# Spectral mixing and a max-of-two MLP: z read back by thirds, exchange reads spread, one batch's stores on SyncE

## The chip, the cores and the metric

The kernel runs on one core of a Trainium2 chip. The metric is the device time of one execution in microseconds. Before the change three runs took 501.76, 507.77 and 511.94 us; their median is 507.77.

The core's engines are TensorE (PE; its weight loads are shown as PEld), VectorE (DVE), ScalarE (ACT), GpSimd (POOL) and SyncE (SP). SyncE computes nothing here: it issues transfers, one after another, in the order in which the program names them, and a transfer that must wait holds up those behind it on that queue.

## The reference

Each of 8 batches of `x` (3072 positions x 256 channels) is transformed along the positions, multiplied by a complex filter and transformed back; every position then passes through an MLP whose hidden value is the larger of two products.

```python
def _attn_ref(x, filt_r, filt_i):
    X = np.fft.rfft(x, axis=1)
    F = (filt_r + 1j * filt_i)[None, :, :]
    Y = X * F
    y = np.fft.irfft(Y, n=x.shape[1], axis=1)
    return y.astype(np.float32)

def _moe_ref(x, w1, w2, w_out):
    h1 = x @ w1
    h2 = x @ w2
    g = np.maximum(h1, h2)
    return (g @ w_out).astype(np.float32)
```

There are 24576 tokens, 256 channels and 1024 hidden units.

## The kernel before, in words

**The transform.** 3072 is 96 x 32, and each batch goes through four small matrix stages with an exchange through DRAM between them. S1 (`s1`, L350) multiplies along 96; its result goes to a DRAM tile `ad` (L372) and comes back in another order as `bt` (`s1_read`, L374: the exchange reads, six per batch, two transfers each). S2 (`s2_pairs`, L445) multiplies along 32; its result times the filter (L464, DVE) is added up to real and imaginary parts on GpSimd (`add_pairs`, L482: L485, L486). S3 (`s3_pairs`, L489) transforms back along 32, in three thirds k = 0, 1, 2 of 8 blocks u each; ACT and DVE copy its result to `zt`, and SyncE writes it to the DRAM tile `zd` with two transfers (L507). The `zd` rows come back in yet another order as `zr`, the z of the change's name (`z_read3`, L381 to L386). S4 (`s4g`, L542, matmuls L549) transforms back along 96. Three tiles of S4 are formed at once: at step 61 of a batch those of the next batch's columns m = 0 to 11, at the next batch's step 4 those of m = 12 to 23, at its step 25 the rest. Each needs all 24 blocks u.

**The MLP.** max(a, b) = b + max(a - b, 0), so one product with w1 - w2 (`Wd`) and a relu do (`moe_h`, L585 to L592), and the w2 branch is folded into a 256 x 256 matrix `M`. `moe_o` (L625) sums ten matmuls per 128 tokens (L640 with `M`, L642 with `Wo`), DVE copies the sum to `ot` (L653), and `out_block` (L597, L601) stores it. `VS` (L580) lists the steps whose relu is on DVE and not on ACT.

**The order.** Everything runs in one schedule written by hand (L912 to L936). A batch is 8 tiles of 384 tokens, a tile has 8 steps, so a batch has 64 steps. At each step TensorE does one of 8 hidden chunks of tile tt (`moe_h`) and about 3 to 7 of the 30 output matmuls of tile tt - 1 (`share`, L896); at some steps a group of transform work for the next batches stands between them (`groups`, L861 to L872: S3 of a third, S2 of a sixth, S1 of some of 8 chunks of x). At a step with a group three of the output matmuls are done ahead of it and the others behind it. `plan(b, step, fn, ...)` hangs a function on the end of a step (`todo`); a step of 64 or more lies in the next batch, a negative one in the batch before. What the functions issue goes to the queues in that order. Batches 1 to 6 (L862) prepare batches 2 to 7 this way; batch 0 prepares batch 1 by other functions.

SyncE's queue in such a batch holds 16 x loads (`load_xf`, L97), 8 S1 writes, 12 exchange reads, 6 z writes, 8 z reads and the stores that GpSimd doesn't issue. x comes into three buffers `XF` in turn; GpSimd adds and subtracts its halves (`fold`, L107, L108), and `load_xf` waits until its buffer has been folded.

**z now.** S3 of the last third is in the group of step 44. `z_read3(b, u0, u1, m)` reads blocks u0 to u1 and 16 of the 32 columns m, in two transfers, one for each s. At step 46 it reads u 0 to 16, at step 47 u 16 to 24, both for m under 16; at steps 54 and 56 the same for m from 16. For u 0 to 16 a transfer has 32 rows of 8 KB (256 KB), for u 16 to 24 it has 16 rows of 8 KB (128 KB).

**Stores now.** Tiles 0 to 7 are stored by GpSimd; of the others up to the last two, the blocks of even number 3 tt + c by GpSimd and those of odd number by SyncE.

Of the kernel before, what the change touches and what calls it, by code (L numbers as in the profile page):

```python
# [13 lines left out]
B = 8  # L14
# [13 lines left out]
def kernel(  # L28
# [14 lines left out]
    nc = tc.nc  # L43
    V, S, G, TE = nc.vector, nc.scalar, nc.gpsimd, nc.tensor
# [276 lines left out]
    zr = {}  # L321
    ad = {}
    zd = {}
# [54 lines left out]
            src = ad[b][48 * r:48 * r + 48].rearrange("(u r) m d -> (r m) u d", r=2)  # L378
            nc.sync.dma_start(out=bt[b][64 * r:64 * r + 64, 4 * v:4 * v + 4], in_=src[:, 4 * v:4 * v + 4])  # L379

    def z_read3(b, u0, u1, m):  # L381
        if b not in zr:
            zr[b] = zrpool.tile([128, NM, D], BF16, tag="zr", name="zr")
        src = zd[b][u0:u1].rearrange("u (s r m) d -> s u r m d", s=2, r=2)
        for s in range(2):
            nc.sync.dma_start(out=zr[b][64 * s + 2 * u0:64 * s + 2 * u1, m:m + 16], in_=src[s][:, :, m:m + 16])  # L386

    def z_read(b, h, ms=(0, 16)):
        if b not in zr:
# [15 lines left out]

    def product(E, v, s, px, pool=None):
        pq = (pool or pqpool).tile([128, 2, 2, D], BF16, tag="pq", name="pq")
        E.tensor_tensor(pq, px.rearrange("p (o i) d -> p o i d", o=1).to_broadcast([128, 2, 2, D]),  # L408
                        F[:, :, 2 * v:2 * v + 2, s], OP.mult)
        return pq  # L410
# [166 lines left out]
            if (j in (1, 4, 6) if 2 < 8 * i + j < 11 else j in (1, 2, 4, 6, 7) if 8 * i + j < 22  # L577
                else (j in (1, 5) and (i, j) != (3, 1)) or (i, j) == (3, 0) if 8 * i + j < 48 else j in (1, 3, 6) and (i, j) != (7, 6))}

    VS = (1, 3, 8, 13, 18, 24, 28, 30, 34, 38, 44, 46, 48, 50, 52, 54, 56, 58, 60)  # L580

    def moe_h(tt, j):
        if j == 0:
# [3 lines left out]
        for dc in range(2):  # L587
            TE.matmul(ph, Wd[:, dc, 128 * j:128 * j + 128], y_[:, dc], start=(dc == 0), stop=(dc == 1))  # L588
        if (tt, j) in on_v if tt < 8 else 8 * (tt % 8) + j in VS if tt < 8 * B - 8 else j in (1, 3, 6):
            V.tensor_scalar(gt[tt][:, j], ph, 0.0, None, OP.max)  # L590
# [6 lines left out]
    def out_block(tt, c):  # L597
        b, i = divmod(tt, 8)
        dst = out[b * N:(b + 1) * N].rearrange("(c p i m) d -> c i p (m d)", c=3, p=32, i=8)[c, i]
        E = G if tt < 8 or (tt < 8 * B - 2 and (3 * tt + c) % 2 == 0) else nc.sync  # L600
        E.dma_start(out=dst, in_=ot[tt // 2][:, 3 * (tt % 2) + c])  # L601


    def last_block(tt):
        y_, g_ = yt[tt], gt[tt]
        dst = out[tt // 8 * N:(tt // 8 + 1) * N].rearrange("(c p i m) d -> c i p m d", c=3, p=32, i=8)[2, tt % 8]
        for cols, E in ((slice(0, 176), S), (slice(176, D), V)):
            pl = ps.tile([128, cols.stop - cols.start], FP32, tag="ps", name="pl")
# [5 lines left out]
            o_ = ot[tt // 2][:, 5, cols]  # L614
            if E is S:
                S.activation(o_, pl, AF.Copy, scale=SCALE)
# [8 lines left out]
    def moe_o(tt, k0, k1):  # L625
        y_, g_ = yt[tt], gt[tt]
        for k in range(k0, k1):
            c, e = divmod(k, 10) if tt else FIRST[k]
            n = e if tt else (e + 2) % 10
            q = 3 * tt + c  # L630
            blk = slice(128 * c, 128 * c + 128)
            if q == 24 * B - 1:
                if e == 0:
                    last_block(tt)
                continue
            if e == 0 and q % 2 == 0:
                po[q // 2 % 2] = pso.tile([128, 2, D], FP32, tag="po", name="po")
            p_ = po[q // 2 % 2][:, q % 2]
            if n < 2:
                TE.matmul(p_, y_[:, n, blk], M[:, n], start=(e == 0), stop=(e == 9))  # L640
            else:
                TE.matmul(p_, g_[:, n - 2, blk], Wo[:, n - 2], start=(e == 0), stop=(e == 9))  # L642
            if e == 9 and q == 24 * B - 2:
                S.activation(ot[tt // 2][:, q % 6], p_, AF.Copy, scale=SCALE)
                out_block(tt, c)
            elif e == 9 and q % 2 == 1:
                if q % 6 == 1:
                    ot[tt // 2] = opool.tile([128, 6, D], FP32, tag="ot", name="ot")
                e = q % 6
                if tt < 8:  # L650
                    V.tensor_copy(ot[tt // 2][:, e - 1:e + 1], po[q // 2 % 2])
                else:
                    V.tensor_scalar(ot[tt // 2][:, e - 1:e + 1], po[q // 2 % 2], SCALE, None, OP.mult)  # L653
                for qq in (q - 1, q):
                    out_block(qq // 3, qq % 3)
# [173 lines left out]
    def plan(b, step, fn, *a):  # L829
        todo.setdefault((b + step // 64, step % 64), []).append((fn, a))  # L830
# [31 lines left out]
    for b in range(1, B - 1):  # L862
        first = b == 1
        plans = [(9, 0, None, (0, 1)), (14, 1, None, (2, 3)), (20, 2, None, (4,)), (30, 3, 0, ()),
                 (34, 4, None, (5, 6)), (38, 5, 1, ()), (44, None, 2, (7,))]
        if first:
            plans = [(10, 0, None, (0, 1)), (15, 1, None, (2,)), (20, 2, None, (3,)), (30, 3, 0, ()),
                     (34, 4, None, (4, 5)), (38, 5, 1, ()), (44, None, 2, (6,)), (50, None, None, (7,))]
        for st, n, k, quads in plans:
            groups[b, st] = (b + 1, n, k, quads)  # L870
            if n is not None and n < 5:
                plan(b, st + 3, add_pairs, b + 1, n)  # L872
        for n, u0, u1, m in ((46, 0, 16, 0), (47, 16, 24, 0), (54, 0, 16, 16), (56, 16, 24, 16)):
            plan(b, n, z_read3, b + 1, u0, u1, m)
        if b + 2 < B:
            xs, folds = (((-30, -23, -9, -3, 4, 11, 18, 25), (-24, -17, -2, 4, 11, 18, 25, 32)) if first
                         else ((-34, -28, -22, -14, -6, 2, 9, 16), range(-22, 34, 7)))
            for c in range(8):
                plan(b, xs[c], load_xf, b + 2, c)
                plan(b, folds[c], fold, b + 2, c)  # L880
            for v, n in enumerate((57, 61, 65, 69, 73, 78) if first else (53, 58, 63, 68, 73, 78)):
                plan(b, n, s1_read, b + 2, v)
    for k, n in enumerate((47, 50, 53, 56, 59)):
        plan(0, n, to_pairs, k)
# [12 lines left out]
    for b in range(B + 1):  # L897
        for i in range(8):
            at = [j for j in range(8) if (b, 8 * i + j) in group or (b, 8 * i + j) in groups]
            if at:  # L900
                n = [6 if j in at else 3 for j in range(8)]
# [3 lines left out]
            else:  # L905
                n = [4, 4, 4, 3, 4, 4, 4, 3]
# [5 lines left out]
    for tt in range(8 * B + 1):  # L912
        b, i = divmod(tt, 8)
        k = 0
        for j in range(8):
# [5 lines left out]
            n = share[b, i][j]  # L921
            if (b, step) in group or (b, step) in groups:
# [5 lines left out]
                k, n = k + 3, n - 3  # L928
# [38 lines left out]
```

## Time and profile before

| | |
|---|---|
| runs | 501.76, 507.77, 511.94 us |
| profiled execution | 509.6 us |
| its span, first to last instruction | 507.8 us |
| mean granted TensorE clock | 0.990 |
| DVE, ACT, POOL busy | 72%, 61%, 59% |
| HBM read, written | 53.87 MB, 47.19 MB |

In the timelines a row gives start and duration in us, engine, line, operation, out<-in and the count of instructions put together in it; what stands in brackets is the engine's idle time ahead of it and what ended that. SPq is SyncE's queue; there the duration includes waiting among the instructions of the row. In the view of waits the three numbers are us in total, times, and the longest in us. In the windows view the columns are the stretch, its length, busy time (and count) of PE, PEld, DVE, ACT and POOL, the granted clock, the mean busy share of the 16 DMA engines, and GB/s.

Batch b begins its step 61, where the first z of the next batch is wanted, at about 158.9 (b = 1), 215.6, 273.0, 336.7 and 395.7 us.

### The profile page before, as it was taken

What the parts mean: (1) busy time and instruction counts of PE and PEld (TensorE: products, weight loads), DVE (VectorE), ACT (ScalarE), POOL (GpSimd) and SP (SyncE); (2) the same over time, 40 slices, a digit from 0 to 9 for tenths busy, and PEclk for the clock granted to TensorE, in tenths of its full rate; (3) what the DMA queues carried; (4) which work ended last, traced back from release to release, by engine and by line L of the source; (5) the groups of instructions that cost most, each with busy time, mean ns of one, the idle gap of its engine ahead of it and who ended that gap; (6) DMA issues with size and microseconds to landing.
All of it is one profiled execution on the core that took longest, in us unless ns stands there. A gap on an engine that the chain in (4) does not pass through costs nothing.

```text
span 507.8 us, 15399 instructions
## 1 busy us (share of the span) xinstructions
PE 484.1 (95%) x6204; PEld 344.2 (68%) x6207; DVE 364.0 (72%) x601; ACT 310.1 (61%) x651; POOL 299.3 (59%) x381
## 2 busy tenths in 40 slices
PE   8689999999899999999998699999999999999997
PEld 3457777776567676767676476766767766777775
DVE  7876787877676878578775487757786788766543
ACT  5777478766564767467764377646774555554432
POOL 8794868558975695749774287755961055311110
PEclk9889999999999999999999899999999999999999
DMA  8999999996688957998589775898657732651212
GB/s 129 155 238 222 252 258 266 274 246 203 168 236 247 243 161 208 273 244 237 153 228 230 170 216 146 236 241 209 201 150 204 209 105 86 187 160 61 72 65 83
DMA packets 85368, 97.37 MB, mean 192 GB/s; under 512 B 8945, under 2 KB 65682, under 8 KB 83922
## 3 DMA queue, kind: packets, MB, share of 16 engines
q1 hardware_dynamic: 75842, 77.34, 56.0%
q0 software_dynamic: 9312, 18.98, 14.9%
q8 instruction: 48, 0.79, 0.7%
q14 instruction: 22, 0.18, 0.1%
q10 hardware_dynamic: 144, 0.09, 0.1%
HBM read 53.87 MB, written 47.19 MB: 199 GB/s over the span
## 4 chain that ended last, share of the span: by engine, by line
PE 61%; DMA 8%; SPq 2%; issue 1%; DVE 0%; ACT 0%; DVEq 0%
PE po L642 24%; PE ph L588 23%; DMA zr<-zd 8%; PE po L640 6%; PE pa L365 2%; PE pz L498 2%; PE px L454 2%; PE pc L549 1%; SPq L386 1%; SPq L601 0%; DVE gt L590 0%; ACT ce L554 0%; PE pl L613 0%; SPq L379 0%; DVE y__9395 L556 0%
## 5 line engine op out<-in xcount | busy, mean ns | idle before, releaser
L642 PE MATMUL po<-Wo,gt 128*128 128x256 bf16 x1528 | 264.1, 274 | 0.0
L592 ACT ACTIVATE gt<-ph 128x384 bf16<-128x384 f32 x352 | 167.9, 502 | 134.3 <-PE ph L588 132.9
L642 PEld LDWEIGHTS <-gt 128*128 128x128 bf16 x1528 | 144.8, 98 | 67.5 <-issue 12.2
L601 POOL DMA_DIRECT2D out_dram<-ot x105 | 59.6, 568 | 137.6 <-DVE ot L653 128.2
L590 DVE TENSOR_SCALAR gt<-ph 128x384 bf16<-128x384 f32 x160 | 88.4, 553 | 48.5 <-PE ph L588 47.3
L588 PEld LDWEIGHTS <-Wd 128*128 128x128 bf16 x1024 | 99.3, 98 | 16.2 <-POOL Wd L301 0.8
L464 DVE TENSOR_TENSOR pf<-px,F 128x1024 f32<-128x1024 f32 x60 | 71.4, 1219 | 24.3 <-PE px L454 9.5
L107 POOL TENSOR_TENSOR xb<-XF 128x512 bf16<-128x512 f32 x48 | 61.1, 1272 | 43.7 <-DMA XF<-in_x_dram 18.9
L653 DVE TENSOR_SCALAR ot<-po 128x512 f32<-128x512 f32 x83 | 56.9, 686 | 20.2 <-PE po L642 19.8
L108 POOL TENSOR_TENSOR xb<-XF 128x512 bf16<-128x512 f32 x48 | 61.7, 1285 | 0.0
L369 ACT ACTIVATE at<-pa 128x512 bf16<-128x512 f32 x96 | 50.7, 606 | 6.7 <-PE pa L365 6.1
L485 POOL TENSOR_TENSOR ri<-pf 128x256 bf16<-128x256 f32 x60 | 43.6, 727 | 9.5 <-DVE pf L464 9.2
L506 ACT ACTIVATE zt<-pz 128x512 bf16<-128x512 f32 x60 | 31.3, 601 | 20.4 <-PE pz L498 20.4
L486 POOL TENSOR_TENSOR ri<-pf 128x256 bf16<-128x256 f32 x60 | 43.4, 723 | 0.0
L554 ACT ACTIVATE ce<-pc 128x384 f32<-128x384 f32 x56 | 24.1, 490 | 13.2 <-PE pc L549 12.0
L408 DVE TENSOR_TENSOR pq<-px,F 128x1024 bf16<-128x1024 f32 x19 | 22.2, 1219 | 4.5 <-PE px L402 2.2
L549 PE MATMUL pc<-G,zr 48*128 48x48 bf16 x896 | 16.5, 181 | 9.3 <-DMA zr<-zd 9.2
L549 PEld LDWEIGHTS <-zr 48*128 48x128 bf16 x896 | 13.5, 93 | 14.6 <-issue 10.1
L365 PE MATMUL pa<-xb,CT 64*32 64x512 bf16 x320 | 17.6, 383 | 0.0
L454 PE MATMUL px<-bt,U 64*32 64x256 bf16 x432 | 14.8, 273 | 0.4 <-DVE gt L590 0.4
L724 PE MATMUL pd<-W 128*128 128x512 bf16 x28 | 9.9, 468 | 1.5 <-DVE zero L153 1.5
L476 DVE TENSOR_TENSOR pf<-px,F 128x512 f32<-128x512 f32 x12 | 8.2, 686 | 4.2 <-issue 4.2
(408 smaller groups left out, 733.7 us busy)
## 6 DMA issues: line engine op xcount, KB each, us to landing
XF<-in_x_dram SPq DMA_DIRECT2D x96, 192.0 KB
out_dram<-ot POOLq DMA_DIRECT2D x105, 128.0 KB, 3.7
out_dram<-ot SPq DMA_DIRECT2D x86, 128.0 KB
ad<-at SPq DMA_DIRECT2D x56, 192.0 KB
zd<-zt SPq DMA_DIRECT2D x42, 256.0 KB
bt<-ad SPq DMA_DIRECT2D x72, 128.0 KB
zr<-zd SPq DMA_DIRECT2D x24, 256.0 KB
zr<-zd SPq DMA_DIRECT2D x24, 128.0 KB
```

What stands on the lines that cost most here:

```text
L107: G.tensor_tensor(t_[:, 0], f[:, 0], f[:, 1], OP.add)
L108: G.tensor_tensor(t_[:, 1], f[:, 0], f[:, 1], OP.subtract)
L369: S.activation(at[:, m0:m0 + 2], pa[g], AF.Copy)
L464: V.tensor_tensor(t_, px[s].rearrange("p (o k) d -> p o k d", o=1).to_broadcast([128, 2, 2, D]), F[:, :, 2 * n, s].rearrange("p c (o d) -> ...
L485: G.tensor_tensor(ri[:, s, 0], t_[:, 0, 0], t_[:, 1, 1], OP.subtract)
L486: G.tensor_tensor(ri[:, s, 1], t_[:, 0, 1], t_[:, 1, 0], OP.add)
L588: TE.matmul(ph, Wd[:, dc, 128 * j:128 * j + 128], y_[:, dc], start=(dc == 0), stop=(dc == 1))
L590: V.tensor_scalar(gt[tt][:, j], ph, 0.0, None, OP.max)
L592: S.activation(gt[tt][:, j], ph, AF.Relu)
L601: E.dma_start(out=dst, in_=ot[tt // 2][:, 3 * (tt % 2) + c])
L642: TE.matmul(p_, g_[:, n - 2, blk], Wo[:, n - 2], start=(e == 0), stop=(e == 9))
L653: V.tensor_scalar(ot[tt // 2][:, e - 1:e + 1], po[q // 2 % 2], SCALE, None, OP.mult)
```

## The change

- `z_read3` takes a third k and a range of columns. The first third is read whole (all 32 columns) at step 39, the second whole at step 47, the last in two halves at steps 51 and 54. There are still 8 transfers per batch, four of 256 KB and four of 128 KB. All have 16 rows now: those of 256 KB have 16 rows of 16 KB.
- S3 of the last third, with the S1 chunk of its group, moves from step 44 to 45, and in `VS` a relu on DVE moves from 44 to 45.
- The exchange reads of batch b + 2 stand at steps 56, 62, 68, 75, 82 and 88 in place of 53, 58, 63, 68, 73 and 78 (batch 1: 57, 61, 65, 69, 73 and 78). They are used at steps 73, 78, 84, 94, 98 and 102.
- Two of the eight x loads of batches 2 on move: -22 to -21 and -14 to -12 (as steps of the batch ahead: 42 to 43 and 50 to 52).
- Stores: tile 7 and all of batch 1's tiles 8 to 15 go to SyncE; from tile 16 on nothing changes.

```diff
-    def z_read3(b, u0, u1, m):
+    def z_read3(b, k, m0, m1):
         if b not in zr:
             zr[b] = zrpool.tile([128, NM, D], BF16, tag="zr", name="zr")
-        src = zd[b][u0:u1].rearrange("u (s r m) d -> s u r m d", s=2, r=2)
+        src = zd[b][8 * k:8 * k + 8].rearrange("u (s r m) d -> s u r m d", s=2, r=2)
         for s in range(2):
-            nc.sync.dma_start(out=zr[b][64 * s + 2 * u0:64 * s + 2 * u1, m:m + 16], in_=src[s][:, :, m:m + 16])
+            nc.sync.dma_start(out=zr[b][64 * s + 16 * k:64 * s + 16 * k + 16, m0:m1], in_=src[s][:, :, m0:m1])
...
-    VS = (1, 3, 8, 13, 18, 24, 28, 30, 34, 38, 44, 46, 48, 50, 52, 54, 56, 58, 60)
+    VS = (1, 3, 8, 13, 18, 24, 28, 30, 34, 38, 45, 46, 48, 50, 52, 54, 56, 58, 60)
...
-        E = G if tt < 8 or (tt < 8 * B - 2 and (3 * tt + c) % 2 == 0) else nc.sync
+        E = G if tt < 7 or (15 < tt < 8 * B - 2 and (3 * tt + c) % 2 == 0) else nc.sync
...
-                 (34, 4, None, (5, 6)), (38, 5, 1, ()), (44, None, 2, (7,))]
+                 (34, 4, None, (5, 6)), (38, 5, 1, ()), (45, None, 2, (7,))]
...
-                     (34, 4, None, (4, 5)), (38, 5, 1, ()), (44, None, 2, (6,)), (50, None, None, (7,))]
+                     (34, 4, None, (4, 5)), (38, 5, 1, ()), (45, None, 2, (6,)), (50, None, None, (7,))]
...
-        for n, u0, u1, m in ((46, 0, 16, 0), (47, 16, 24, 0), (54, 0, 16, 16), (56, 16, 24, 16)):
-            plan(b, n, z_read3, b + 1, u0, u1, m)
+        for n, k, m0, m1 in ((39, 0, 0, 32), (47, 1, 0, 32), (51, 2, 0, 16), (54, 2, 16, 32)):
+            plan(b, n, z_read3, b + 1, k, m0, m1)
...
-                         else ((-34, -28, -22, -14, -6, 2, 9, 16), range(-22, 34, 7)))
+                         else ((-34, -28, -21, -12, -6, 2, 9, 16), range(-22, 34, 7)))
...
-            for v, n in enumerate((57, 61, 65, 69, 73, 78) if first else (53, 58, 63, 68, 73, 78)):
+            for v, n in enumerate((56, 62, 68, 75, 82, 88)):
```

## The prediction

> **What bounds the kernel now.** I read the page first: TensorE is busy 95% of the span, the chain that ended last is TensorE's for three fifths, and after TensorE its largest part is one transfer, the read of z back from DRAM.
>
> ```profile
> span 507.8 us, 15399 instructions
> ...
> PE 484.1 (95%) x6204; PEld 344.2 (68%) x6207; DVE 364.0 (72%) x601; ACT 310.1 (61%) x651; POOL 299.3 (59%) x381
> ...
> PE 61%; DMA 8%; SPq 2%; issue 1%; DVE 0%; ACT 0%; DVEq 0%
> ```
>
> So only a stop of TensorE can be won. The view of waits, for TensorE alone, says what ends its stops:
>
> ```profile
> PE pc L549 <- DMA zr<-zd: 9.2, 8, 2.5
> ...
> PE pz L498 <- POOL ri L485: 1.1, 1, 1.1
> ...
> PE pz L498 <- POOL ri L486: 0.4, 1, 0.4
> ...
> PE px L454 <- DVE gt L590: 0.4, 1, 0.4
> ```
>
> Third, TensorE's timeline where the z matmuls of L549 stand (batches 1 and 2, then 3, then 4; a batch's first three tiles are formed at step 61, the next three at step 68, which is step 4 of the next batch):
>
> ```profile
> 158.88 0.77 PE L549 MATMUL pc<-G,zr 48*128 48x48 bf16 x48
> ...
> 165.66 0.56 PE L549 MATMUL pc<-G,zr 48*128 48x48 bf16 x31 [0.46 <-DMA zr<-zd]
> ```
> ```profile
> 215.59 0.77 PE L549 MATMUL pc<-G,zr 48*128 48x48 bf16 x48
> ...
> 222.94 0.56 PE L549 MATMUL pc<-G,zr 48*128 48x48 bf16 x31 [1.03 <-DMA zr<-zd]
> ```
> ```profile
> 272.96 0.19 PE L549 MATMUL pc<-G,zr 48*128 48x48 bf16 x1
> 274.46 0.75 PE L549 MATMUL pc<-G,zr 48*128 48x48 bf16 x47 [1.31 <-DMA zr<-zd]
> ...
> 282.28 0.18 PE L549 MATMUL pc<-G,zr 48*128 48x48 bf16 x1 [1.54 <-DMA zr<-zd]
> 285.00 0.56 PE L549 MATMUL pc<-G,zr 48*128 48x48 bf16 x31 [2.54 <-DMA zr<-zd]
> ```
> ```profile
> 336.72 0.18 PE L549 MATMUL pc<-G,zr 48*128 48x48 bf16 x1
> 338.02 0.77 PE L549 MATMUL pc<-G,zr 48*128 48x48 bf16 x47 [1.12 <-DMA zr<-zd]
> ...
> 344.94 0.19 PE L549 MATMUL pc<-G,zr 48*128 48x48 bf16 x1 [0.62 <-DMA zr<-zd]
> 345.73 0.57 PE L549 MATMUL pc<-G,zr 48*128 48x48 bf16 x31 [0.60 <-DMA zr<-zd]
> ```
>
> The eight gaps sum to 9.22 us, the whole of the first row above. 2.43 us of it (1.31 and 1.12) is at step 61, which wants columns m under 12; 6.79 us is at step 68, which wants m from 16 on. Batch 2's step 61 got through without a gap. After the stop that ended at 285.00 the granted clock falls; stretches of time, 4 us each:
>
> ```profile
> 285.00:289.00 4.00, 4.00 (x46) 2.69 (x47) 1.95 (x4) 1.85 (x4) 2.18 (x2) 0.57 0.75 198
> ```
>
> At 0.57 for 4 us that is 4 x 0.43 = 1.7 us more, bought by two long stops in a row (1.54 and 2.54).
>
> **Why z is late.** SyncE issues nearly all transfers in one order. Its queue at the end of batches 1, then 2 and 3, then 4:
>
> ```profile
> 146.75 0.95 SPq L507 DMA_DIRECT2D zd<-zt  x2
> 147.80 0.59 SPq L601 DMA_DIRECT2D out_dram<-ot  x1
> 148.50 5.44 SPq L386 DMA_DIRECT2D zr<-zd  x4
> ```
> ```profile
> 152.52 0.69 SPq L386 DMA_DIRECT2D zr<-zd  x1
> ```
> ```profile
> 203.91 0.95 SPq L507 DMA_DIRECT2D zd<-zt  x2
> ...
> 261.17 0.94 SPq L507 DMA_DIRECT2D zd<-zt  x2
> ...
> 263.70 1.96 SPq L601 DMA_DIRECT2D out_dram<-ot  x1
> 265.76 2.88 SPq L386 DMA_DIRECT2D zr<-zd  x4
> ```
> ```profile
> 324.91 1.09 SPq L507 DMA_DIRECT2D zd<-zt  x2
> ```
>
> In batch 1 the last z write is issued by 147.70, the third of the four reads (the first that needs that write) starts only at 152.52: 4.8 us from write to landing, in which the queue stands still. That the first two reads went out at 148.50 shows that a read waits for its own rows only, so the new read of the first third at step 39 will not wait for later thirds. From issue to landing a z read takes, in the chain of waits:
>
> ```profile
> 159.88 5.65 DMA zr<-zd
> ...
> 216.96 5.85 DMA zr<-zd
> ...
> 267.96 6.37 DMA zr<-zd
> ...
> 275.76 9.11 DMA zr<-zd
> ...
> 331.50 6.48 DMA zr<-zd
> ```
>
> These are queueing times: where they fall, the DMA engines are nearly full (last but one column, share busy):
>
> ```profile
> 260.30:273.00 12.70, 12.67 (x103) 9.48 (x99) 7.20 (x14) 5.74 (x13) 9.08 (x9) 1.00 0.92 248
> 273.00:285.00 12.00, 6.61 (x105) 4.94 (x106) 6.18 (x12) 4.32 (x10) 3.63 (x4) 1.00 0.97 214
> ```
>
> **The change, part by part.** The sum is made against the profiled execution, 509.6 us (span 507.8, 1.8 around it), which is 0.4% above the median of 507.77.
>
> *Step 68 (m from 16).* Now its last reads are emitted at step 56, behind the four of steps 46 and 47, an x load, two exchange reads and two more z reads. After the change the last are two of 128 KB at step 54, with one x load between them and step 51's, and the exchange reads of step 53 come behind them at 56. So they land two or three transfers after step 61's own, while step 68 wants them 6.3 us after step 61 (158.88 to 165.2 in batch 1, its gap of 0.46 taken off). All 6.79 us go, and with the stops at 282.28 and 285.00 the clock's 1.7. Without that cover, at the landing times below, they would stay at most.
>
> *Step 61 (m under 12).* Here the change adds lateness. S3 of the last third moves from step 44 to 45. The mean step is 56.7 / 64 = 0.89 us (158.88 to 215.59 is a batch); a step without a group is shorter, and I take 0.7. Its read moves from 46/47 to 51, by when the queue has nothing left to do but wait for the write to land (4.8). The second of the two reads starts 0.7 later (0.69 in the row at 152.52), and then comes the landing. Per batch, from the end of the writes' issue: batch 1: 147.70 + 0.7 + 4.8 = 153.2, the second read starts at 153.9, + 5.65 = 159.6, wanted at 158.88: 0.7 late. Batch 2: 204.86 gives 210.4, then 211.1, + 5.85 = 217.0 against 215.59: 1.4. Batch 3: 262.11 gives 267.6, then 268.3, + 6.37 = 274.7 against 273.1 (its second z matmul, the first that waits): 1.6. Batch 4: 326.00 gives 331.5, then 332.2, + 6.48 = 338.7 against 336.9: 1.8. Batches 5 and 6 have fewer loads beside them and no z stop now; I take nothing there. Sum 5.5 us; with no load at all in the queues it is 0, and the other end is in the next part. Behind the read that waits on SyncE stand an x load, the reads of step 54 and a store; the reads have the 6.3 us of step 68, and nobody wants the others within 5 us.
>
> *The bytes ahead of it.* The reads of the second third (step 47) have 16 rows of 16 KB where two of the old four had 32 rows of 8 KB. What a 16-row read costs the queue shows where two of them issued 0.7 us apart end stops one after the other: 0.79 us (344.94 to 345.73) and 2.72 us (282.28 to 285.00), for half the bytes. Two reads at twice the bytes so add between 2 x 0.79 = 1.6 and 2 x 2.72 = 5.4 us; they start about 1.4 us sooner, since the store that held the queue for 1.96 us at 263.70 is now emitted ahead of S3 (at step 45 the tile's second block is complete in the three matmuls before the group). Net 0.2 to 4.0 us a batch. I take 0.8, with 1.1 a read, nearer the calm row, because the third now read at step 39 has left the full stretch. Four batches: 3.2 us.
>
> *Batch 1's stores.* 15 blocks (one batch's 12 even ones and 3 of tile 7) go from GpSimd to SyncE, 15 x 0.59 = 8.9 us of queue. Four fall into the full stretch from 145 on, 2.4 us; against them stand two reads gone to step 39 and the standstill of 148.50 (5.44 for four reads instead of some 2.9). Each waits for the same copy as the store beside it. Taken as nothing; without that cover 2.4 us. GpSimd gains:
>
> ```profile
> 121.41 0.56 POOL L601 DMA_DIRECT2D out_dram<-ot  x1 [1.25 <-DVE ot L653]
> ...
> 132.96 0.56 POOL L601 DMA_DIRECT2D out_dram<-ot  x1
> ...
> 136.00 0.72 POOL L485 TENSOR_TENSOR ri<-pf 128x256 bf16<-128x256 f32 x1
> ```
>
> It works without a break from 121.41 to the sums at 136.00 that TensorE waits for (1.1 + 0.4, and 0.4 for the engine behind them). Three stores (1.7 us) and one wait (1.25) leave: all 1.9 us go. At worst, if the vector engine's products are late next, 0.
>
> *The rest.* Exchange reads come up to 10 steps later (the last at step 88, used at 102): 14 mean steps are 12.4 us, the longest landing above is 9.11, so nothing; with SyncE 4 us behind at the time, a stop of 1 us. Loads shifted by one or two steps, and one relu changed from DVE to ACT and one back: nothing.
>
> *Sum.* 509.6 - 9.2 - 1.7 - 1.9 = 496.8, the floor; + 5.5 + 3.2 = **505.5**.
>
> **Rivals.** *All z stops go:* if landings shorten by 1.5 us because two of eight reads leave the full stretch (512 KB at 248 GB/s are 2.1 us), step 61 is on time: 496.8 to 498, say 497.5. Against it: the read must still wait for its write, and batch 2 had no slack to give 0.7 us away.
>
> *The thirds jam (slower).* If every 16-row read costs what the busy row shows, 2.72 us, each of four batches is 4.0 later: 5.5 + 16 = 21.5, and single stops of 5 us bring the clock down, 1.7 in three batches: 496.8 + 21.5 + 5.1 = 523. It decides from 5.3 us of loss per batch over four batches (518). For it: the full DMA share; the new reads at 39 also stand before the last z write. Against: 2.72 was seen once. [...]
>
> *The change does nothing to z:* the reads bunch behind the same late queue and stops only change place: 509.6 - 1.9 = 507.7.
>
> **How the numbers follow.** Forecast 0.45 (501 to 512 by its own terms), all stops gone 0.2, jam 0.25, nothing 0.1. Two per cent of 507.77, about what a measurement of this kernel can tell from no change, are the limits 497.6 and 517.9. The first rival straddles the lower one, and better luck at the start may help: faster 0.2; jam slower 0.25; the rest 0.55. Range 498 to 519.
>
> **What would show it.** Right: no gap before the second group of L549 in any batch; a single gap of 1 to 3 us before the first, in batches 1 to 4, ended by DMA zr<-zd; no gap at S3 near 138; clock 1.00 after 290. SyncE waits for zd<-zt ahead of the reads of step 51. Wrong: gaps over 4 us at step 61 with landings over 7 us, or none at all, or stops for bt or ri in their place.

## The result, and the profile after

The changed kernel takes 543.15 us (median of 6 runs, 540.33 to 544.54) against 507.91 for the kernel before beside it (6 runs): ratio 1.074, 95% interval 1.067 to 1.080. It is slower by 35 us, where 505.5 was forecast and 519 was the end of the range. Here and below the medians are over all runs, while the ratios leave out runs more than 1.5% above the fastest of the same kernel, so the two can differ by up to 0.7%. The profiled execution took 540.33 us. Its page, the span first, then TensorE, the chain that ended last, and the row of S4's matmuls (busy, mean of one, then the idle time ahead of them); the last line is that row on the page of the kernel before:

```profile
span 538.6 us, 15373 instructions
...
PE 492.7 (91%) x6207; PEld 348.7 (65%) x6207; DVE 363.8 (68%) x601; ACT 310.3 (58%) x651; POOL 290.0 (54%) x366
...
PE 74%; DMA 18%; POOL 3%; issue 2%; SPq 2%; DVE 1%; ACT 1%; POOLq 0%; DVEq 0%
...
L549 PE MATMUL pc<-G,zr 48*128 48x48 bf16 x896 | 18.0, 189 | 33.8 <-DMA zr<-zd 20.9
```
```profile
L549 PE MATMUL pc<-G,zr 48*128 48x48 bf16 x896 | 16.5, 181 | 9.3 <-DMA zr<-zd 9.2
```

The idle time is the result in short: TensorE stands 33.8 us before S4, where it stood 9.3 in all (9.2 of them for z). The span has grown by 538.6 - 507.8 = 30.8 us: 33.8 - 9.3 = 24.5 of waiting, and 492.7 - 484.1 = 8.6 of busy time, for the same matmuls. The sum is 2.3 too large; 1.5 of that is the stop for GpSimd near 138 (1.1 + 0.4) that has gone.

TensorE's timeline, the first z group of each batch (step 61; small windows of it; in batch 1 also its second row), and the first row of step 68 in batch 1:

```profile
162.48 0.22 PE L549 MATMUL pc<-G,zr 48*128 48x48 bf16 x1 [5.90 <-DMA XF<-in_x_dram]
163.67 1.14 PE L549 MATMUL pc<-G,zr 48*128 48x48 bf16 x47 [0.97 <-DMA zr<-zd]
...
170.89 0.77 PE L549 MATMUL pc<-G,zr 48*128 48x48 bf16 x48
...
227.82 0.20 PE L549 MATMUL pc<-G,zr 48*128 48x48 bf16 x1 [6.71 <-DMA zr<-zd]
...
291.41 0.20 PE L549 MATMUL pc<-G,zr 48*128 48x48 bf16 x1 [5.48 <-issue]
...
356.36 0.22 PE L549 MATMUL pc<-G,zr 48*128 48x48 bf16 x1 [6.13 <-DMA zr<-zd]
...
417.75 0.19 PE L549 MATMUL pc<-G,zr 48*128 48x48 bf16 x1 [2.65 <-DMA zr<-zd]
...
477.47 0.20 PE L549 MATMUL pc<-G,zr 48*128 48x48 bf16 x1 [3.11 <-DMA zr<-zd]
```

All six batches stop at step 61, four of them for about 6 us; step 68, where 6.79 us were lost before, passes (the row at 170.89 has no bracket). Two of the names in brackets mislead: a matmul of L549 has G and zr as its inputs, so neither a transfer of x (162.48) nor nothing at all ("issue", 291.41) can have held it; it is z in all six. The six stops sum to 29.98 us; a second, shorter one stands behind the first matmul in every batch (0.97 us in batch 1, 0.35 to 0.79 in the others), and with these it is the 33.8 of the page, all of it at step 61. The busy time that was added is the clock. Windows around the first stop (length, busy PE, PEld, DVE, ACT, POOL, then the granted clock, DMA share, GB/s):

```profile
156.58:162.48 5.90, 0.00 (x1) 0.01 (x1) 0.69 (x1) 0.19 (x1) 0.00 (x0) 0.78 0.70 194
159.85:166.68 6.83, 3.23 (x57) 2.35 (x58) 1.99 (x5) 1.49 (x4) 0.93 (x1) 0.50 0.75 215
166.68:173.51 6.83, 6.74 (x95) 4.90 (x94) 4.25 (x9) 3.97 (x10) 4.07 (x4) 1.00 0.61 177
```

The clock is granted at half from 159.85 to 166.68, 4.2 us of it after TensorE has its first data. While the stop lasts the 16 DMA engines are 70% busy (the 0.70 of the first row) and not full.

SyncE's queue in the same batch:

```profile
144.24 1.52 SPq L386 DMA_DIRECT2D zr<-zd  x2
145.86 0.85 SPq L97 DMA_DIRECT2D XF<-in_x_dram  x2
146.81 2.18 SPq L601 DMA_DIRECT2D out_dram<-ot  x2
149.08 1.15 SPq L507 DMA_DIRECT2D zd<-zt  x2
150.28 3.50 SPq L386 DMA_DIRECT2D zr<-zd  x2
153.88 1.23 SPq L601 DMA_DIRECT2D out_dram<-ot  x2
155.21 0.99 SPq L372 DMA_DIRECT2D ad<-at  x2
156.33 1.46 SPq L386 DMA_DIRECT2D zr<-zd  x2
```

The first third's read, planned for step 39, leaves at 144.24, when TensorE is at step 45: it stands behind stores that wait for the vector engine (one of them 2.0 us, in the view of waits). The last z write goes at 149.08, in place of 146.75. The second third's two reads need 3.50 us; the last third's are issued at 156.33 and 157.09, and step 61 wants them at 156.58 (162.48 - 5.90). What held the second third's, in the view of waits for SyncE in 140 to 165:

```profile
SPq L386 <- DMA zr<-zd: 2.1, 1, 2.1
...
SPq L97 <- DMA zr<-zd: 1.3, 2, 1.1
```

A read of z, and then loads of x, wait for the landing of other reads of z: a transfer here is not issued before the eighth before it on the queue has landed (the one of 153.08 followed on a landing at 153.06; all 438 that have an eighth ahead of them start behind its landing, by 0.016 us at the least). In batch 2 the write itself is the last to end; the chain of waits has its landing, 8.75 us after issue, and right behind it the read's:

```profile
212.35 8.75 DMA zd<-zt
...
221.89 6.46 DMA zr<-zd
```

The landing of every transfer of SyncE's queue stands in the trace as the last step of its semaphore. All 446 of the change land in the order of their issue (of the 431 of the kernel before two land behind the next one, by 0.07 and 0.53 us). So a pair of z reads can be given the time from the landing of the transfer ahead of it to its own last landing (a wait ahead of the issue counts in it too). In the kernel before, the two pairs that step 61 wants take 4.0 to 5.2 us together in a batch; in the change the three pairs take 11.9 to 13.3 (in batch 1 7.39, 3.39 and 2.51). The last write is issued behind the first third's read and lands behind it, and in all six batches the last third's read is issued within 0.3 us of that landing.

### The profile page after: what moved, and what is told of

It is laid out like the page before. It is cut to its first block, busy times and chain, and to the rows that moved or that the text cites. A ratio compares the mean times of both kernels' runs of the same rounds, so it can differ in the third digit from the quotient of the medians.

```text
span 538.6 us, 15373 instructions
## 1 busy us (share of the span) xinstructions
PE 492.7 (91%) x6207; PEld 348.7 (65%) x6207; DVE 363.8 (68%) x601; ACT 310.3 (58%) x651; POOL 290.0 (54%) x366
## 4 chain that ended last, share of the span: by engine, by line
PE 74%; DMA 18%; POOL 3%; issue 2%; SPq 2%; DVE 1%; ACT 1%; POOLq 0%; DVEq 0%
PE po L642 28%; PE ph L588 27%; DMA zr<-zd 9%; PE po L640 7%; DMA zd<-zt 5%; DMA xb<-in_x_dram 3%; PE pc L549 3%; PE pa L365 2%; PE pz L498 2%; PE px L454 2%; POOL pq L408 1%; SPq L386 1%; POOL xb L92 1%; PE pz L426 1%; DMA F<-in_filt_r_dram 1%
## 5 line engine op out<-in xcount | busy, mean ns | idle before, releaser
L642 PE MATMUL po<-Wo,gt 128*128 128x256 bf16 x1528 | 267.6, 277 | 0.0
L642 PEld LDWEIGHTS <-gt 128*128 128x128 bf16 x1528 | 147.5, 99 | 69.9 <-issue 14.1
L601 POOL DMA_DIRECT2D out_dram<-ot x90 | 51.0, 568 | 150.5 <-DVE ot L653 132.4
L588 PEld LDWEIGHTS <-Wd 128*128 128x128 bf16 x1024 | 100.5, 99 | 17.3 <-DVE y__4747 L556 0.4
L549 PE MATMUL pc<-G,zr 48*128 48x48 bf16 x896 | 18.0, 189 | 33.8 <-DMA zr<-zd 20.9
L549 PEld LDWEIGHTS <-zr 48*128 48x128 bf16 x896 | 15.0, 98 | 39.2 <-DMA zr<-zd 17.7
L365 PE MATMUL pa<-xb,CT 64*32 64x512 bf16 x320 | 16.3, 383 | 0.0
```

What stands on the lines that cost most here:

```text
L549: TE.matmul(pc[s][k][:, dc, m], zr[b][64 * s:64 * s + 48, 4 * i + m, 128 * dc:128 * dc + 128], G2[64 * s:64 * s + 48], start=True, stop=True)
```

## The experiments

Ratios are against runs of the kernel before on the same chip, with 95% intervals. "Wait at S4" is the idle time in the page's row for S4's matmuls, the 9.3 and 33.8 of above.

### Which part of the change: z alone, or all but z

The kernel before with the new `z_read3` and its plan line and nothing else; and the changed kernel with the old ones back:

```diff
# z only (on before); the reverse edit on after is "all but z"
...
+        for n, k, m0, m1 in ((39, 0, 0, 32), (47, 1, 0, 32), (51, 2, 0, 16), (54, 2, 16, 32)):
-        for n, u0, u1, m in ((46, 0, 16, 0), (47, 16, 24, 0), (54, 0, 16, 16), (56, 16, 24, 16)):
...
```

> Before plus only the reads of z by thirds (steps 39, 47, 51, 54; S3 stays at step 44). Theory E (a transfer with 8 blocks outermost runs on half of the DMA engines, so that all z reads crowd there): nearly the whole loss returns, 530 to 545 us, with stops of 4 to 7 us at step 61 of each batch and z landings over 5 us even where little else moves. Theory R (the other edits, SyncE's 15 stores and the later exchange reads, make the loss): 505 to 512. Theory T (only the step from 44 to 45 makes the last third late): 503 to 508, stops at step 61 under 1 us.

> The changed kernel with the old four reads of z (steps 46, 47, 54, 56) put back; all its other edits stay. E: 503 to 512, near the kernel before. R: 535 to 545. T: S3 at step 45 makes step 61 late by 1 to 3 us a batch, 510 to 520.

z alone: 551.99 us, ratio 1.089 (1.082 to 1.096), wait at S4 42.2 us: longer than any of the three theories had it. All but z: 503.67 us, ratio 0.997 (0.993 to 1.001), with

```profile
span 498.1 us, 15376 instructions
...
L549 PE MATMUL pc<-G,zr 48*128 48x48 bf16 x896 | 16.0, 180 | 4.3 <-DMA zr<-zd 4.3
```

The reading by thirds carries the whole loss. The rest is no worse than before, and it takes about 9 us off the loss that z alone makes (551.99 to 543.15). The last z write moved to step 45 stands in "all but z" too and costs nothing that can be seen.

### Which engines carry a read

A second copy of the rows' order in DRAM, so that a third's 16 rows are one dimension of 16 and not 8 x 2; this takes twelve z writes in place of six.

```diff
-            zd[b] = dram.tile([NU, 128, D], BF16, tag="zd", name="zd")
+            zd[b] = dram.tile([2, NU, 64, D], BF16, tag="zs", name="zd")
...
-        src = zd[b][8 * k:8 * k + 8].rearrange("u (s r m) d -> s u r m d", s=2, r=2)
...
+            src = zd[b][s, 8 * k:8 * k + 8].rearrange("u (r m) d -> (u r) m d", r=2)
```

> The changed kernel with z kept in DRAM as two halves by s, so that the 16 rows of a third are one dimension of 16 in the source too; same bytes, same rows of 8 or 16 KB, same partitions, same steps. The z writes are twice as many of half the size (6 more issues a batch on SyncE). E: the reads spread over all engines, 500 to 512 us, stops at step 61 under 2 us. Theory L (rows of 16 KB, or their 16 partitions, are slow on any engines): as the changed kernel, 535 to 548, stops of 4 to 7 us. T: stops of 1 to 3 us, 506 to 516.

538.53 us, ratio 1.062 (1.056 to 1.068): 5 us of 35. The traces show the difference: a z read of the changed kernel raises its semaphore in 9 steps, one of this kernel in 16, like the x loads, stores and writes of the queue. (In the kernel before, the 24 reads with 8 blocks outermost have 9 steps and the 24 with 16 blocks have 16. No row names the engine of a packet.) The same shapes were then measured alone, in a kernel that leaves out all the reference's work: 16 reads of a kind at a time, into eight tiles in pairs, a copy by DVE as each pair lands.

> Not the reference's work: only reads of z from DRAM with nothing beside them, 16 transfers of one shape in a row, then a copy of each of 8 tiles by the vector engine; six shapes, twice. Shapes: 32 rows of 8 KB; 16 rows of 8 KB; 16 rows of 16 KB; the same with the rows as one dimension of 16 in DRAM; 32 rows of 16 KB; 16 rows of 8 KB as one dimension. 16 issues take some 11 us by themselves. E: 16 rows of 16 KB take about as long as 32 rows of 16 KB with twice the bytes (20 to 40 us), and the merged rows half of that or the 11 us of the issues. L: 16 KB rows take as long merged or not.

DVE's timeline in that kernel; the distance from row to row is what a pair takes. Rows 46.36 and 48.38 are the last third's read of before and after (16 rows of 8 KB), 63.00 and 67.54 the new whole third (16 rows of 16 KB), 183.31 and 185.02 the last third from the copy with 16 rows outermost, 195.26 and 197.45 the old two thirds (32 rows of 8 KB), 264.47 and 268.74 the whole third from that copy, 290.23 and 294.91 two whole thirds in one (32 rows of 16 KB):

```profile
46.36 0.20 DVE L61 COPY acc<-zr 128x32 bf16<-128x32 bf16 x1 [1.82 <-DMA zr<-zd]
48.38 0.19 DVE L61 COPY acc<-zr 128x32 bf16<-128x32 bf16 x1 [1.82 <-DMA zr<-zd]
...
63.00 0.19 DVE L61 COPY acc<-zr 128x32 bf16<-128x32 bf16 x1 [4.42 <-DMA zr<-zd]
67.54 0.20 DVE L61 COPY acc<-zr 128x32 bf16<-128x32 bf16 x1 [4.35 <-DMA zr<-zd]
...
183.31 0.19 DVE L61 COPY acc<-zr 128x32 bf16<-128x32 bf16 x1 [1.53 <-DMA zr<-zs]
185.02 0.19 DVE L61 COPY acc<-zr 128x32 bf16<-128x32 bf16 x1 [1.52 <-DMA zr<-zs]
...
195.26 0.19 DVE L61 COPY acc<-zr 128x32 bf16<-128x32 bf16 x1 [2.03 <-DMA zr<-zd]
197.45 0.19 DVE L61 COPY acc<-zr 128x32 bf16<-128x32 bf16 x1 [1.99 <-DMA zr<-zd]
...
264.47 0.19 DVE L61 COPY acc<-zr 128x32 bf16<-128x32 bf16 x1 [4.07 <-DMA zr<-zs]
268.74 0.19 DVE L61 COPY acc<-zr 128x32 bf16<-128x32 bf16 x1 [4.07 <-DMA zr<-zs]
...
290.23 0.20 DVE L61 COPY acc<-zr 128x32 bf16<-128x32 bf16 x1 [4.46 <-DMA zr<-zd]
294.91 0.19 DVE L61 COPY acc<-zr 128x32 bf16<-128x32 bf16 x1 [4.49 <-DMA zr<-zd]
```

So a pair takes 2.0 us (narrow third), 4.55 (whole third), 2.2 (old two thirds), 1.7 and 4.3 (narrow and whole third, 16 outermost) and 4.7 (two whole thirds at once). By these rows the rate goes with the number of rows of a read: a whole third and the old two thirds carry the same 512 KB in times that differ by two, 115 GB/s for 16 rows (524288 bytes in 4.55 us) and 238 for 32. The 9 or 16 steps, 4.55 us against 4.3, hardly count.

This kernel alone doesn't settle it. It does everything twice, and the rows shown of the narrow and of the whole thirds are of its first round, those of the old two thirds of its second. In the second round the narrow thirds took 1.25 us a pair and the whole ones 2.4 to 3.6 (some 210 GB/s at the best); in both rounds the whole ones took up to 7.5 and 9.1 with the reads of the next kind under way beside them. The sums by pairs measured alone in the table below therefore stand for the slow first round of the thirds. In the kernels themselves, by the landings, it is nearer the slow end: in the kernel before, the narrow pair takes 1.9 to 3.3 us in batches 1 to 4 where the pair of 32 rows, with twice the bytes, takes 1.8 to 3.0; in the change the second whole third takes 3.4 to 4.8. The forecast's rival, with 2.72 us a read, had about the right price.

### Is it the neighbouring rows?

A second kernel that leaves out all the reference's work puts the 16 rows on other rows of the tile.

> Not the reference's work: reads of z alone, 16 in a row, as before, six shapes of 16 rows: a third as the changed kernel reads it (16 neighbouring partitions); the same into every third of 48 partitions; that with the rows as one dimension of 16 in DRAM; 8 KB rows into every third partition; a third into partitions 0 to 15 and 16 to 31 in turn; into 0 to 15 and 32 to 47 in turn. Theory P (16 neighbouring partitions take in only some 115 GB/s, whatever engines send): spread 256 KB in 1.1 to 1.4 us each where neighbours take 2.3; 0 to 15 with 16 to 31 like the first shape or faster, 0 to 15 with 32 to 47 not faster than 2.2. Theory N (16 rows are slow wherever they lie): all 16 KB shapes 2.1 to 2.3. E (half the engines): spread 2.3, spread with one dimension of 16 1.1.

Its copies by DVE: rows 45.00 and 49.54 whole thirds as in the change, 57.11 and 60.36 the same on every third row, 150.21 and 155.29 both of a pair on rows 0 to 15 and 32 to 47 in place of 0 to 15 and 64 to 79:

```profile
45.00 0.19 DVE L61 COPY acc<-zr 128x32 bf16<-128x32 bf16 x1 [4.32 <-DMA zr<-zd]
49.54 0.19 DVE L61 COPY acc<-zr 128x32 bf16<-128x32 bf16 x1 [4.35 <-DMA zr<-zd]
...
57.11 0.19 DVE L61 COPY acc<-zr 128x32 bf16<-128x32 bf16 x1 [2.89 <-DMA zr<-zd]
60.36 0.19 DVE L61 COPY acc<-zr 128x32 bf16<-128x32 bf16 x1 [3.06 <-DMA zr<-zd]
...
150.21 0.19 DVE L61 COPY acc<-zr 128x32 bf16<-128x32 bf16 x1 [4.96 <-DMA zr<-zd]
155.29 0.19 DVE L61 COPY acc<-zr 128x32 bf16<-128x32 bf16 x1 [4.88 <-DMA zr<-zd]
```

4.5, 3.2 and 5.1 us a pair: where the rows lie in the tile matters. (Of the shapes not shown, rows 0 to 15 with 16 to 31 took 3.1 to 4.3, narrow reads on every third row 1.1 to 1.7, some 1.3.) The 512 KB of a pair go into 16 neighbouring rows at 115 GB/s, into every third row of 48 at 164, and into 32 neighbouring rows, in the kernel above, at 238. Why 16 neighbouring rows are the slower ones no run shows. In the kernel, each third's rows on every third row, with the table G permuted to match:

```diff
-            nc.sync.dma_start(out=zr[b][64 * s + 16 * k:64 * s + 16 * k + 16, m0:m1], in_=src[s][:, :, m0:m1])
+            nc.sync.dma_start(out=zr[b][64 * s + k:64 * s + 48:3, m0:m1], in_=src[s][:, :, m0:m1])
...
```

> The changed kernel with the rows of a third put on every third of the 48 partitions (and the rows of the S4 table in the same order); reads, bytes, steps and engines as in the changed kernel. P: the landing time of the thirds falls to that of 32 rows, 498 to 510 us, stops at step 61 under 2 us. N and E: 535 to 548, stops of 4 to 7.

528.24 us, ratio 1.042 (1.033 to 1.050), wait at S4 19.7: it takes 15 of the 35 us away, between the 498 to 510 of theory P and the 535 and more of the others. The other 20 stay with the rows spread this way, at which a pair still takes 3.2 us alone.

### Fewer or smaller transfers

The plan line alone (and the reads written by blocks u0 to u1, as before): first two thirds read together, whole, at step 42; and each third in two reads of 8 KB rows.

```diff
+        for n, u0, u1, m0, m1 in ((42, 0, 16, 0, 32), (51, 16, 24, 0, 16), (54, 16, 24, 16, 32)):
# and, in the other kernel:
+        for n, u0, u1, m0, m1 in ((39, 0, 8, 0, 16), (39, 0, 8, 16, 32), (47, 8, 16, 0, 16), (47, 8, 16, 16, 32), (51, 16, 24, 0, 16), (54, 16, 24, 16, 32)):
```

> The changed kernel with the first two thirds read together at step 42 (two transfers of 512 KB, 32 rows of 16 KB); the last third as in the changed kernel. P and N: z takes 2.3 us for 512 KB in place of 4.6, and the last third is small: 500 to 512, stops at step 61 of 0 to 2 us. L (16 KB rows): 525 to 545.

> The changed kernel with each third in two reads of 8 KB rows (12 transfers a batch, all of 128 KB, into 16 neighbouring partitions). P: 128 KB take 0.6 to 1.0 us alone against 2.3 for 256 KB, so between: 515 to 540, stops of 2 to 6 us. L: 500 to 510.

536.22 us, ratio 1.058 (1.051 to 1.066), and 538.49, ratio 1.063 (1.056 to 1.069). The first falls where theory L put it, that rows of 16 KB are slow; the second, with rows of 8 KB, rules L out. Nor is it the number of transfers: 12 small ones cost no more than 8. Common to all the slow versions is what is read before step 61: all 32 columns of two thirds, half of which only step 68 wants.

### What stands ahead of step 61

The thirds as they are, but only the first 16 columns ahead of step 61; the same with the rows spread; the old two reads with the first moved to step 42; and the first two thirds' reads issued by GpSimd.

```diff
# thirds, first columns only
+        for n, u0, u1, m0, m1 in ((39, 0, 8, 0, 16), (47, 8, 16, 0, 16), (51, 16, 24, 0, 16), (54, 0, 16, 16, 32), (56, 16, 24, 16, 32)):
# the same, spread
+        for n, k, m0, m1 in ((39, 0, 0, 16), (47, 1, 0, 16), (51, 2, 0, 16), (54, 0, 16, 32), (55, 1, 16, 32), (56, 2, 16, 32)):
# old reads, first one early
+        for n, u0, u1, m0, m1 in ((42, 0, 16, 0, 16), (47, 16, 24, 0, 16), (54, 0, 16, 16, 32), (56, 16, 24, 16, 32)):
# changed kernel, two thirds by GpSimd
+            (nc.sync if k == 2 else G).dma_start(out=zr[b][64 * s + 16 * k:64 * s + 16 * k + 16, m0:m1], in_=src[s][:, :, m0:m1])
```

> The changed kernel with each third read in its first 16 columns only ahead of step 61 (steps 39, 47, 51), the other 16 columns of thirds 0 and 1 together at step 54 and of third 2 at step 56. Theory B (bytes and rows ahead: the transfers that stand ahead of step 61's data are paid one after another at the rate of their rows; by the transfers measured alone, a pair of 16-row 16 KB reads takes 4.5 us, a pair of 16-row 8 KB reads 2.0, so 4.5 + 4.5 + 2.0 = 11.0 us ahead of step 61 in the changed kernel, 6.0 here, 4.1 with the old four reads): the five first gaps of about 6 us shrink by up to 5 us each, to 1 to 2 us, the clock stays at 1.0 in most batches, and the time is 508 to 518 us. Theory T (third 2 or its writer comes too late, whatever stands ahead): the gaps stay at 5 to 6 us, 535 to 545 us. Theory W (the queue holds 8 transfers at once): as many transfers ahead of step 61 as before, so half of the loss at least stays: 525 to 540 us.

> As the kernel with thirds on every third row, and with only the first 16 columns of each third ahead of step 61. Theories B and P together (by the transfers measured alone a pair of 16-row 8 KB reads on every third row takes 1.3 us, so 3.9 us ahead of step 61, as few as the 4.1 of the old four reads): the stops at step 61 go down to 1 us or less and the time is 500 to 508 us, level with the old reads. If something else in the reading by thirds costs (number of transfers, the waits for the third's writes): 512 us or more.

> The changed kernel with two reads as the old ones in shape (thirds 0 and 1 together, 16 columns, 32 rows; then third 2), the first at step 42 instead of 46, the second at step 47, the late columns at 54 and 56. Theory B: 4.1 us ahead of step 61, half of it issued earlier: 498 to 505 us, no stop over 1 us at step 61. Theory T (an early read that waits for its writer holds up the store and the operand read behind it on SyncE): 505 to 515 us, with stops elsewhere.

> The changed kernel with the reads of thirds 0 and 1 issued from GpSimd's queue, so that SyncE's queue neither waits for their writers nor counts them among its transfers under way. Theory W (SyncE's queue is held by the transfers under way and by the waits of the early reads): the read of third 2 leaves some 3 to 5 us earlier, the stops at step 61 fall to 1 to 3 us, 510 to 525 us. Theory B: the bytes still share the same rows, third 2 lands as late as before, 535 to 545 us; GpSimd's own work stops behind the waits and can add a stop at its groups.

Thirds with first columns only: 516.15 us, ratio 1.019 (1.012 to 1.026), wait at S4 13.6: 27 of the 35 us gone by 512 KB a batch that come later. Spread as well: 512.34, ratio 1.011 (1.004 to 1.018), a miss of its 500 to 508. Early old reads: 511.36, ratio 1.010 (1.006 to 1.014), a miss too, and slower than the same reads at 46. Its trace says why; SyncE's queue there, and then in the kernel with all but z:

```profile
144.06 1.27 SPq L386 DMA_DIRECT2D zr<-zd  x2
...
147.81 1.59 SPq L507 DMA_DIRECT2D zd<-zt  x2
153.55 1.51 SPq L386 DMA_DIRECT2D zr<-zd  x2
```
```profile
146.97 2.35 SPq L507 DMA_DIRECT2D zd<-zt  x2
149.41 3.97 SPq L386 DMA_DIRECT2D zr<-zd  x4
```

With the early read ahead of it, the last write is issued at 147.81 and 148.93 and the last third's read can follow only at 153.55; without, the write goes at 146.97 and 147.60 and the four reads are all out by 153.38. The read sent ahead of the last write delayed that write's landing, which is what the last read waits for: the last of the writes lands at 153.50 there, and at 151.91 without the early read.

By GpSimd: 531.65 us, ratio 1.051 (1.044 to 1.058), wait at S4 25.5. It gains 11 us, less than the 18 and more that a queue held by transfers under way was to bring, and more than nothing. No transfer of SyncE's queue waits for a read of z near batch 1's step 61 any more. Yet the last write, issued by 150.88, lands at 156.96 (156.08 in the change): in batch 1 the last third's read goes at 157.09, no earlier than in the change, and GpSimd stands still for the write before its own read:

```profile
149.18 1.09 POOL L386 DMA_DIRECT2D zr<-zd  x2 [7.31 <-DMA zd<-zt]
```

### Each suspect alone, added to the good reads

On the changed kernel, four plan lines that part from the two good ones by one thing each: thirds of first columns with the last read at 47; the old reads with the second at 51; the old reads with the first widened to all columns; the old reads with the first cut in two.

```diff
# thirds of first columns, last read at 47
+        for n, u0, u1, m0, m1 in ((39, 0, 8, 0, 16), (45, 8, 16, 0, 16), (47, 16, 24, 0, 16), (54, 0, 16, 16, 32), (56, 16, 24, 16, 32)):
# old reads, second at 51
+        for n, u0, u1, m0, m1 in ((46, 0, 16, 0, 16), (51, 16, 24, 0, 16), (54, 0, 16, 16, 32), (56, 16, 24, 16, 32)):
# old reads, first one widened
+        for n, u0, u1, m0, m1 in ((46, 0, 16, 0, 32), (47, 16, 24, 0, 16), (56, 16, 24, 16, 32)):
# old reads, first one cut in two
+        for n, u0, u1, m0, m1 in ((46, 0, 8, 0, 16), (46, 8, 16, 0, 16), (47, 16, 24, 0, 16), (54, 0, 16, 16, 32), (56, 16, 24, 16, 32)):
```

> The kernel with thirds in their first 16 columns ahead of step 61, with the last third's read at step 47 in place of 51 (third 1's at 45 in place of 47). Theory T: the last read leaves some 3 us earlier (at about 152 of the trace, as with the old reads, in place of 154.9), the remaining stops of 2.0 to 2.4 us at step 61 go to under 1 us, no slow clock after them, 502 to 508 us. Theory N (the cut into thirds, with its rows in two transfers, is the rest): 512 to 518 us, as it was.

> The changed kernel with the old four reads, and only the second of them (third 2, 16 columns) at step 51 in place of 47. Theory T: the read leaves 2 to 3 us later, behind step 48's store and the operands for the exchange, and step 61 stops for 1.5 to 2.5 us in each of the five batches, with half a slow window of the clock behind it: 510 to 518 us. Without T: 502 to 506 us, as with the old reads.

> The changed kernel with the old four reads, and only the first of them widened from 16 to all 32 columns (so that of the late reads one is left out). Theory B: by the transfers measured alone a pair of 32-row reads takes 4.7 us with 16 KB rows and 2.2 us with 8 KB rows, so step 61's last data lands 2.5 us later, stops of 2 to 3 us in five batches: 512 to 522 us. If early bytes are not what costs: 500 to 507 us.

> The changed kernel with the old four reads, and only the first of them cut into two of 16 rows each, at the same step. Theory N: two pairs of 16-row 8 KB reads take 2.0 us each where the pair of 32 rows took 2.2, so 1.8 us more ahead of step 61: stops of about 2 us, 508 to 515 us. Without N (the read of third 1 waits little, and the third's rows land while the last third is still being written): 501 to 507 us.

The table has all the kernels of these experiments but the two that measure reads alone, and the change. "Alone" adds, for the reads ahead of step 61, the pairs measured alone; "landed" is the same in the kernel's own trace, by the landings as above, the mean of six batches.

| kernel | us | ratio | alone, us | landed, us |
|---|---|---|---|---|
| all but z (old reads) | 503.67 | 0.997 (0.993 to 1.001) | 2.2 + 2.0 = 4.2 | 4.6 |
| second old read at 51 | 506.51 | 1.000 (0.997 to 1.003) | 4.2 | 4.9 |
| old reads, first at 42 | 511.36 | 1.010 (1.006 to 1.014) | 4.2 | 7.9 |
| thirds, first columns, last at 47 | 510.57 | 1.011 (1.006 to 1.016) | 3 x 2.0 = 6.0 | 8.0 |
| thirds, first columns, on every third row | 512.34 | 1.011 (1.004 to 1.018) | 3 x 1.3 = 3.9 | 7.2 |
| first old read cut in two | 512.01 | 1.012 (1.007 to 1.017) | 6.0 | 6.7 |
| thirds, first columns, last at 51 | 516.15 | 1.019 (1.012 to 1.026) | 6.0 | 8.4 |
| first old read widened | 521.51 | 1.022 (1.018 to 1.027) | 4.7 + 2.0 = 6.7 | 8.0 (in the run of 526.34) |
| thirds on every third row | 528.24 | 1.042 (1.033 to 1.050) | 2 x 3.2 + 1.3 = 7.7 | 10.1 |
| two whole thirds by GpSimd | 531.65 | 1.051 (1.044 to 1.058) | 11.1 | in two queues |
| two whole thirds at once, at 42 | 536.22 | 1.058 (1.051 to 1.066) | 4.7 + 2.0 = 6.7 | 10.4 |
| thirds, 16 rows outermost | 538.53 | 1.062 (1.056 to 1.068) | 2 x 4.3 + 1.7 = 10.3 | 10.4 |
| thirds in 8 KB rows | 538.49 | 1.063 (1.056 to 1.069) | 5 x 2.0 = 10.0 | 11.6 |
| the change | 543.15 | 1.074 (1.067 to 1.080) | 2 x 4.55 + 2.0 = 11.1 | 12.7 |
| z alone | 551.99 | 1.089 (1.082 to 1.096) | 11.1 | 13.3 |

(The 1.3 is a pair of narrow reads on every third row.) The pairs measured alone give the order roughly. Three kernels are slower than their sum: the old reads with the first at 42, the first columns on every third row, and the two whole thirds at once. The landings in the kernel's own trace, in which a wait for the last write counts, put these three in place too. This last column comes from the same executions as the stops; it says where the time goes and doesn't predict it.

By the ratios, against the 0.997 of the first line and at 507.9 us, widening one read (and leaving out the later read of the same columns) costs 13 us (0.025 x 507.9); cutting one in two with the same bytes costs about 7; the later place of the last read alone costs 1.5, which the intervals don't tell from nothing. The kernel with one read cut and the one with thirds at 39, 45 and 47 agree (512.01 and 510.57): reading the first third seven steps earlier brings nothing that can be measured.

## Why the prediction was wrong, step by step

**What bounds the kernel, and step 68:** right. All 6.79 us at step 68 went, as said: its reads landed 1.2 to 3.7 us behind step 61's, within the 6.3 that the forecast gave them. TensorE's stops, and the clock behind them, are what the time is made of (24.5 and 8.6 us of its growth, as above).

**GpSimd, batch 1's stores, exchange reads:** nothing speaks against it. The stop near 138 went, and no stop for `bt` or a store came in its place in the change. That these edits gain the 1.9 us is not shown: all but z is 1.5 us faster by its ratio, with an interval that holds nothing as well. No experiment took these three apart.

**"Step 61":** this is where it failed. The term was 0.7 to 1.8 us a batch, 5.5 in all; measured are 5.90, 6.71, 5.48 and 6.13 in batches 1 to 4 (24.2), and 2.65 and 3.11 in batches 5 and 6, for which nothing was taken (the second, shorter stops left out). Batch 2 shows it by the step's own terms: the write's landing was put at 4.8 us and took 8.75, the read's at 5.85 and took 6.46. In batch 1 the second read was to start at 153.9 and started at 157.09, while TensorE arrived at 156.58 in place of 158.88. The step kept the landing times of the old queue; since the transfers landed in the order of their issue (all 446), the new reads ahead of the write and behind it lengthened both. (The 5.65 us that it took for batch 1 were those of step 68's read; step 61's had landed in 3.56.)

**"The bytes ahead of it":** the mechanism was named, the size was wrong, and so was the place. It counted only the second third's reads, at 1.1 us each, "because the third now read at step 39 has left the full stretch". It has not: it was issued at step 45, ahead of the last write. A pair of whole thirds takes 4.55 us alone and not 2.2, and two pairs stand ahead, 9.1 in place of the old 2.2; in the kernel they took 10.5 to 11.7. The row that showed 2.72 us for a 16-row read, set aside because it was seen once, was nearer to the 2.3 that 16 KB rows take alone than the 1.1 of the sum.

**Clock:** the forecast had none of it behind step 61. Six stops brought six windows at half clock, where the kernel before had one near 285, and 8.6 us of added busy time.

**The rival that jams** had the side right, and about its price per read (2.72 us, where 2.3 was measured alone). Theory E, which the experiments asked about first, explains little of that price: with 16 rows outermost a pair of reads takes 4.3 us and not 4.55, and the kernel 538.5 and not 543. The rival stopped at 523 because it took four batches and 4.0 us each.

**What stays open:** how the loss divides among the parts. SyncE's wait for the eighth transfer before did not itself hold the read that ended last: in every batch that read was issued within 0.3 us of the landing of its write, and the write was issued ahead of the wait. What the wait costs by way of the second third's reads is not taken apart. Spreading the rows took 15 us away and issuing from GpSimd 11, but that edit also makes GpSimd wait, and the two may overlap. Why the thirds ran at two rates when measured alone (4.55 and 2.4 to 3.6 us a pair of whole ones) is not known. Taking only the place of the last read off the thirds gave 516.15 to 510.57, with intervals that touch.

## What to carry to other kernels

A read moved ahead of a write was paid by that write here (its landing went from 151.91 to 153.50 with the early read): before splitting a read to start parts of it early, ask what the part that ends last waits for, and what now stands ahead of that. Order reads by who wants them first, and count their cost by the rows that they fill and not by their bytes alone (512 KB alone took 4.55 us into 16 rows a read in the first round, 2.2 into 32). A plan's step is not the time of issue (the read of step 39 left at step 45): look in the queue for what the transfer stands behind.

## What the runs showed of the hardware that was not expected

- Reads into 16 neighbouring rows ran at 115 to 130 GB/s with 16 KB and with 8 KB rows (4.55 and 2.0 us a pair) in the first round of the measurement, and at up to twice that in the second, for which no cause was found; into 32 rows at 238 (8 KB) and 224 (16 KB), into 16 rows three apart at 164.
- A stop of about 6 us (batches 1 to 4) comes with half a clock for 6.83 us, which begins before the stop has ended; so does the one of 3.11 us, while 3.41 us of it followed the one of 2.65. The six windows added 8.6 us of busy time to that of the kernel before, which had one of 3.41 us in its batches.
- Transfers of SyncE's queue landed in the order of their issue (all 446 of the change), whatever they carried. Two loads of x behind the first third's reads took 7.6 us to land, and 3.6 to 4.5 a little earlier.
- SyncE's queue issued nothing while the eighth transfer back hadn't landed (438 of 438 in the change, 423 of 423 before), so slow landings delayed transfers that have nothing to do with them: two loads of x waited 1.3 us for reads of z.
